# The second layer's two products: one loop over token spans, against two phases with the hidden values stored in DRAM between them

## The chip, the cores and the metric

The program runs on one core of a Trainium2 chip. The core has a matrix engine (TensorE, PE in the rows, with its weight loads as PEld), a vector engine (VectorE, DVE), a scalar engine (ScalarE, ACT), GpSimd (POOL) and the sync engine (SP), which issues the transfers between DRAM and on-chip memory. The metric is the device time in microseconds (us) of one execution.

## The reference, cut to what matters

```
x = attention(q, k, v)                   # 8 batches x 576 tokens; x is 4608 tokens x 512
h = maximum(x @ w1_in, 0);  x2 = (h * h) @ w1_out         # first layer, hidden width 2048
h = x2 @ w2_in;  g = maximum(0.01 * h, h)                 # second layer, hidden width 2048
out = g @ w2_out                                          # 4608 x 512
```

Only the last two lines are computed differently by the changed kernel. The weights arrive as 64-bit floats, and earlier code turns them into 32-bit words.

## The kernel before, in words

Every product is made of three passes in the PE's reduced 32-bit format: a value is rounded to a high part (a ScalarE copy), the low part is the difference (a VectorE subtraction), and high x high, low x high and high x low are added up in PSUM. I call the two steps "high" and "low" below.

The attention and the first layer run in blocks of 512 tokens. A background helper, `Stored`, converts the second layer's weights at the same time, a step per `tick` (L335), and stores them in DRAM: `w2_raw` for `w2_in`, and `w2_parts`, already split in high and low, for `w2_out`. The first layer's result goes to DRAM as `x2`.

The second layer (`Second`) starts when the last block of the first ends. A span is 768 tokens, seen as two halves of 384. Its first product is a Strassen-Winograd scheme: the 512 input columns, the 256 hidden columns of a "pair" and the 768 tokens are each cut in two, and 7 block products take the place of 8. `x_sum`, `x_high` and `x_low` make the 7 forms of x for a span, on tiles of 128x768; `make_in` makes the 7 forms of the weights of a pair. A group is one pair on one span: `product(g, j)` (L1310) is 6 matmuls of 384 columns, and `use` (L1328) drains it. The drains alternate over two PSUM banks, and product j accumulates on top of product j - 2, so it can start only when the drain of j - 2 has read the bank.

After each of the products 0 to 5 stands one `piece` (L1378) of the group before: 6 matmuls of 512 columns, for 128 tokens, of the second product. The leaky relu is a VectorE operation (L1358), and then high (L1362) and low (L1365) of the hidden values follow. On-chip memory holds the weights of 4 of the 8 pairs, so the spans are walked twice, forward for pairs 0 to 3 and backward for 4 to 7, and the result of the first walk goes through DRAM (`part`). That is 48 groups in all. When the span changes, the forms of the next span are made during the last pair (p = 3) and the first steps of the next group, one form after each product.

The order of the instructions on each engine is the order in which the code issues them; nothing reorders it. SP issues its transfers in that order too, at most 8 of them outstanding.

Of the kernel before, what the change touches and what calls it, by code (L numbers as in the profile page):

```python
# [43 lines left out]
def attention_relu2_leaky_kernel(  # L44
# [67 lines left out]
    w2_parts = dram.tile([FC // 2, P, 2, 1024], F32, tag="w2p", name="w2p")  # L112
    part = dram.tile([NT, DM], F32, tag="part", name="part")
# [101 lines left out]
    def half_words_of(w, kind, i, n):  # L215

        if kind == 0:
            src = w[2 * n * P : 2 * (n + 1) * P, 4 * i * P : 4 * (i + 1) * P]
            return (
                src.rearrange("(k p) f -> p k f", p=P),  # L220
                lambda t: t.rearrange("p (k f) w -> p k (f w)", k=2),
            )
        c = 2 * i + n
        return w[c * P : (c + 1) * P, :], lambda t: t.rearrange("p f w -> p (f w)")
# [94 lines left out]
    class Stored:  # L319
# [8 lines left out]
        def load(self, h):  # L328
            kind, i, n = h % 2, h // 4, h // 2 % 2
            src, to = half_words_of(self.w[kind], kind, i, n)  # L330
            t = sb([P, 512, 2], U32, "val")
            nc.sync.dma_start(out=to(t), in_=src)
            self.halves[h] = t[:, :, 0], t[:, :, 1]

        def tick(self):  # L335
# [18 lines left out]
            elif k == 4 and h % 2:  # L354
                t = sb([P, 2, 512], F32R, "val")
                nc.vector.tensor_copy(t[:, 0, :], self.out)
                nc.vector.tensor_tensor(
                    out=t[:, 1, :], in0=self.out, in1=f32(t[:, 0, :]), op=ALU.subtract
                )
                self.out = f32(t)  # L360
            elif k == 5 - (h + 1) % 2:
                i, n = h // 4, h // 2 % 2
                to = w2_parts[i, :, :, n * 512 : (n + 1) * 512] if h % 2 else w2_raw[i, :, n]
                nc.sync.dma_start(out=to, in_=self.out)
# [786 lines left out]

    TS = 384
    SPAN = 2 * TS
    SPANS = NT // SPAN
    TT = SPAN // P
    PAIRS = FC // 4
    A11, A12, A22, S1, S2, S3, S4 = range(7)
    FORMS = (A11, S2, A12, S3, S1, A22, S4)

    class Second:  # L1160
        def __init__(self):
            self.order = [(0, n) for n in range(SPANS)] + [(1, n) for n in reversed(range(SPANS))]
            self.groups = [(*o, p) for o in self.order for p in range(PAIRS)]
            self.weights, self.outs, self.late, self.begun = {}, {}, [], {}

        def open_forms(self):
# [3 lines left out]
            opened.insert(0, pool)  # L1170
# [7 lines left out]
        def open_work(self):  # L1178
            pool = tc.alloc_tile_pool(name="gs", bufs=1, side="right", reuse_waits="tile")
            opened.append(pool)  # L1180
            self.gh, self.gl = (
                [
                    [
                        [pool.tile([P, TS], F32R, tag=f"{n}{k}{c}{t}", name=n) for t in range(2)]
                        for c in range(2)
                    ]
                    for k in range(2)
                ]
                for n in ("sh", "sl")
            )  # L1190
            POOLS.update({"u3": pool, "h11": pool})
            BUFS.update({"u3": 2, "h11": 2})
            self.acc = [acc_bank(m) for m in range(KC)] + [bank() for _ in range(2)]
            self.banks = [bank() for _ in range(2)]
# [37 lines left out]
        def load_in(self, half, p):  # L1232
            i = PAIRS * half + p
            self.words = [sb([P, 2, 2, P], F32, "raw") for _ in range(2)]
            for n, t in enumerate(self.words):
                nc.sync.dma_start(out=t.rearrange("p k j f -> p (k j f)"), in_=w2_raw[i, :, n])

        def make_in(self, p):
            ra, rb = self.words
            sums = sb([P, 4, 2, P], F32, "sums")  # L1240
            s1, s2, s3, s4 = (sums[:, n] for n in range(4))
            hi = sb([P, 7, 2, P], F32R, f"wi{2 * p}")
            lo = sb([P, 7, 2, P], F32R, f"wi{2 * p + 1}")
# [25 lines left out]
        def fetch_out(self, half, p):  # L1269
# [226 lines left out]
```

## Time and profile before

| | us |
|---|---|
| median of 3 runs (1725.42 to 1729.01) | 1728.6 |
| the profiled execution | 1730.24 |
| its span, from first to last instruction | 1728.5 |
| PE busy in the span | 1695.7 |
| VectorE busy | 1110.4 |
| ScalarE busy | 626.5 |

The span is the time from the first to the last instruction; the execution takes 1.7 us more. The granted clock of the PE is 0.997 of full speed. The matmuls overlap, so a single one's length in the rows (337 ns for 384 columns) is longer than the step from one start to the next, and it is the steps that add up. The second layer takes the stretch from 979 us to the end.

### The profile page before, as it was taken

What the parts mean: (1) busy time and instruction counts of PE and PEld (TensorE: products, weight loads), DVE (VectorE), ACT (ScalarE), POOL (GpSimd) and SP (SyncE); (2) the same over time, 40 slices, a digit from 0 to 9 for tenths busy, and PEclk for the clock granted to TensorE, in tenths of its full rate; (3) what the DMA queues carried; (4) which work ended last, traced back from release to release, by engine and by line L of the source; (5) the groups of instructions that cost most, each with busy time, mean ns of one, the idle gap of its engine ahead of it and who ended that gap; (6) DMA issues with size and microseconds to landing.
All of it is one profiled execution on the core that took longest, in us unless ns stands there. A gap on an engine that the chain in (4) does not pass through costs nothing.

```text
span 1728.5 us, 21707 instructions
## 1 busy us (share of the span) xinstructions
PE 1695.7 (98%) x8312; PEld 1465.9 (85%) x8312; DVE 1110.4 (64%) x2020; ACT 626.5 (36%) x1496; POOL 19.4 (1%) x38
## 2 busy tenths in 40 slices
PE   6999999999999999999999999999999999999999
PEld 6778888888888888888888899999999999999997
DVE  7978886667656676665435565565566675666564
ACT  4545343343443433433433332332332332233221
POOL 0011000000000000000000000000000000000000
PEclk9999999999999999999999999999999999999999
DMA  8924542322223232232004202201202411330220
GB/s 224 336 93 162 173 135 95 101 97 95 77 100 109 85 98 79 83 113 74 19 29 161 80 1 74 74 16 58 74 31 92 171 60 51 110 109 8 104 74 37
DMA packets 106296, 162.44 MB, mean 94 GB/s; under 512 B 44112, under 2 KB 44240, under 8 KB 105168
## 3 DMA queue, kind: packets, MB, share of 16 engines
q1 hardware_dynamic: 103632, 152.67, 26.3%
q0 software_dynamic: 2560, 8.39, 1.3%
q8 instruction: 65, 1.06, 0.2%
q14 instruction: 39, 0.32, 0.1%
HBM read 111.75 MB, written 49.28 MB: 93 GB/s over the span
## 4 chain that ended last, share of the span: by engine, by line
PE 91%; DVE 4%; ACT 2%; DMA 2%; issue 1%; SPq 1%; DVEq 0%
PE acc L910 21%; PE ps L1317 20%; PE ps L872 17%; PE acc L1384 15%; PE ps L1384 8%; PE acc L872 4%; PE ps L587 2%; PE ps L650 1%; DMA wo<-in_moe_w_out 1%; DMA wi<-in_moe_w_in 1%; PE ps L551 1%; PE acc L381 1%; ACT s L608 1%; DVE xl L679 0%; PE ps L656 0%
## 5 line engine op out<-in xcount | busy, mean ns | idle before, releaser
L872 PE MATMUL ps<-xh,wi 128*128 128x512 f32 x896 | 296.5, 393 | 0.0
L1317 PE MATMUL ps<-fh,wi 128*128 128x384 f32 x1344 | 289.2, 337 | 0.1
L910 PE MATMUL acc<-gh,wo 128*128 128x512 f32 x1080 | 276.7, 394 | 0.7 <-ACT xl L882 0.7
L1317 PEld LDWEIGHTS ps<-fh,wi 128*128 128x128 f32 x1344 | 243.1, 188 | 22.2 <-DVE gh L1330 0.4
L910 PEld LDWEIGHTS acc<-gh,wo 128*128 128x128 f32 x1080 | 200.7, 189 | 41.8 <-ACT xl L882 1.2
L1384 PE MATMUL acc<-wo,sh 128*128 128x512 f32 x768 | 205.6, 390 | 0.0
L872 PEld LDWEIGHTS ps<-xh,wi 128*128 128x128 f32 x896 | 168.2, 188 | 34.6 <-issue 0.2
L872 PE MATMUL ps<-xl,wi 128*128 128x512 f32 x448 | 174.4, 389 | 0.0
L1317 PE MATMUL ps<-fl,wi 128*128 128x384 f32 x672 | 171.2, 336 | 0.0
L889 DVE CAST gh<-r 128x512 fp32r<-128x512 f32 x112 | 47.6, 425 | 174.5 <-ACT r L885 173.9
L1384 PEld LDWEIGHTS acc<-wo,sh 128*128 128x128 f32 x768 | 141.5, 188 | 15.6
L910 PE MATMUL acc<-gl,wo 128*128 128x512 f32 x540 | 149.6, 391 | 0.0
L882 ACT ACTIVATE r<-ps 128x512 f32<-128x512 f32 x112 | 67.7, 605 | 208.9 <-PE ps L872 204.6
L1317 PEld LDWEIGHTS ps<-fl,wi 128*128 128x128 f32 x672 | 121.4, 188 | 0.0
L1384 PE MATMUL acc<-wo,sl 128*128 128x512 f32 x384 | 120.3, 392 | 0.0
L910 PEld LDWEIGHTS acc<-gl,wo 128*128 128x128 f32 x540 | 101.8, 189 | 21.6
L608 ACT ACTIVATE s<-ps,m 128x72 f32<-128x72 f32 x240 | 72.1, 330 | 93.8 <-DVE m L599 93.7
L1330 DVE TENSOR_TENSOR u<-gh,ps 128x384 f32<-128x384 f32 x48 | 26.6, 554 | 120.1 <-PE ps L1317 120.1
L1384 PE MATMUL ps<-wo,sh 128*128 128x512 f32 x384 | 102.8, 390 | 0.0
L872 PEld LDWEIGHTS ps<-xl,wi 128*128 128x128 f32 x448 | 84.2, 188 | 16.5
L1384 PEld LDWEIGHTS acc<-wo,sl 128*128 128x128 f32 x384 | 72.0, 188 | 18.3 <-DVE sl L1365 3.7
L890 DVE TENSOR_TENSOR gl<-r,gh 128x512 fp32r<-128x512 f32 x112 | 77.6, 692 | 7.8 <-PE ps L656 0.5
(211 smaller groups left out, 2419.8 us busy)
## 6 DMA issues: line engine op xcount, KB each, us to landing
wi<-in_moe_w_in SPq DMA_DIRECT2D x8, 1024.0 KB
wo<-in_moe_w_out SPq DMA_DIRECT2D x8, 1024.0 KB
val<-in_moe_w_in SPq DMA_DIRECT2D x16, 512.0 KB
val<-in_moe_w_out SPq DMA_DIRECT2D x16, 512.0 KB
w2p<-val SPq DMA_DIRECT2D x16, 512.0 KB
wo<-w2p SPq DMA_DIRECT2D x8, 1024.0 KB
xh<-x SPq DMA_DIRECT2D x10, 768.0 KB
xl<-x SPq DMA_DIRECT2D x10, 768.0 KB
```

Source lines behind the costliest of these rows:

```text
L381: nc.tensor.matmul(ps[:n, c * 2 * D : (c + 1) * 2 * D], lhsT=ident[:n, :n], rhs=raw[:n, r * 2 * D : (r + 1) * 2 * D], start=r == 0, stop=r ...
L551: nc.tensor.transpose(ps[:, cc * P : (cc + 1) * P], raw[:, cc * P : (cc + 1) * P], ident)
L587: nc.tensor.matmul(ps[: r0 + n, c2 * PAIR : (c2 + 1) * PAIR], lhsT=qt[:, cc, : r0 + n], rhs=kts[b][:, keys], start=True, stop=True,)
L608: nc.scalar.activation(out=s[:, g, :], in_=ps[:, h * SP : (h + 1) * SP], func=AF.Exp, bias=m[:, g : g + 1], accum_out=None if i in early e ...
L872: nc.tensor.matmul(ps, lhsT=w[:, kc], rhs=x[kc], start=(kc == 0 and n == 0), stop=(kc == KC - 1 and n == 2),)
L882: nc.scalar.activation(out=r, in_=ps, func=AF.Relu)
L889: nc.vector.tensor_copy(gh, r)
L890: nc.vector.tensor_tensor(out=gl, in0=r, in1=f32(gh), op=ALU.subtract)
L910: nc.tensor.matmul(acc[m], lhsT=w[:, m * P : (m + 1) * P], rhs=x, start=(c == 0 and n == 0), stop=(c == FC - 1 and n == 2),)
L1317: nc.tensor.matmul(at, lhsT=w[:, FORMS[j], kc], rhs=x[j][:, kc], start=m == 0 and j in (0, 1, 4), stop=m == 5, skip_group_check=True,)
L1330: nc.vector.tensor_tensor(out=out_, in0=x, in1=at, op=ALU.add)
L1384: nc.tensor.matmul(self.acc[i], lhsT=x[g % 2][c][t][:, at], rhs=self.outs[p][:, part_, c], start=p == 0 and m == 0, stop=p == PAIRS - 1 an ...
```

## The change

The second layer is done in two phases. In phase 1 the six spans are walked once, over all 8 pairs (48 groups, p = 0 to 7), with the first product alone. The weights of pairs 4 to 7 go to the tiles of the first layer's `w_out`, and are made during the first five groups. The drains use two sets of three PSUM banks, set by set in turn. The leaky relu becomes ScalarE's Lrelu. No high and low of the hidden values are made here: five forms of them, two of which are sums made by VectorE (`sums_of`), go to DRAM (`h_forms`), 5 transfers of 192 KB a group.

In phase 2 the second product is a 7-product scheme too: hidden rows, the two token halves, and the two halves of the 512 output columns are cut. A round is 256 columns of the 2304-wide forms; 9 rounds of 8 groups are walked. A group loads 5 forms (640 KB), VectorE makes the other two, ScalarE makes the high and VectorE the low of all seven, and the PE does 7 products of 6 matmuls with 256 columns. The products accumulate over the 8 groups of a round in 7 of the 8 PSUM banks, and are drained in the last group of a round.

The forms of `w_out` are made by `Stored` (`w2_forms`, in place of `w2_parts`), loaded in the last span of phase 1 and split there, a pair per group, behind product 1 (`split_out`).

```diff
@@ Stored.tick, half of w_out
-                t = sb([P, 2, 512], F32R, "val")
-                nc.vector.tensor_copy(t[:, 0, :], self.out)
-                nc.vector.tensor_tensor(
-                    out=t[:, 1, :], in0=self.out, in1=f32(t[:, 0, :]), op=ALU.subtract
...
+                nc.sync.dma_start(out=to[:, 0:1], in_=o[:, 0, 0:1])
+                nc.sync.dma_start(out=to[:, 1:3], in_=o[:, 1])
+                t = sb([P, 4, P], F32, "val")
+                for at, x, y in (
+                    (t[:, 0:2], o[:, :, 1], o[:, 0]),
...
+            elif k == 5 and h % 2:
+                t, to = self.sums
+                nc.sync.dma_start(out=to[:, 3:7], in_=t)
@@ product, use
-            at = self.banks[(g + j) % 2][:, :TS]
+            at = self.banks[3 * (g % 2) + (0, 1, 0, 1, 2, 1, 2)[j]][:, :TS]
...
+            def leaky(out_, x):
+                nc.scalar.activation(out=out_, in_=x, func=AF.Lrelu)
...
-                self.leaky(self.u2, k, 0, 1)
-
-        def leaky(self, h, k, c, t):
-            nc.vector.scalar_tensor_tensor(
-                out=h, in0=h, scalar=0.01, in1=h, op0=ALU.mult, op1=ALU.max
-            )
...
+                leaky(self.u2, self.u2)
+                self.late.append(self.sums_of(g))
+
+        def sums_of(self, g):
...
+                s3 = sb([P, TS], F32, "st")
+                nc.vector.tensor_tensor(out=s3, in0=h11, in1=h21, op=ALU.subtract)
+                nc.vector.tensor_tensor(out=h21, in0=h21, in1=h22, op=ALU.add)
+                for at, x in ((H11, h11), (H12, h12), (H22, h22), (HS3, s3), (HS1, h21)):
+                    nc.sync.dma_start(out=to[:, at], in_=x)
@@ group
+                at = self.product(g, j)
+                if more and p == PAIRS - 2 and j in (1, 2, 4):
                     self.x_sum((1, 2, 4).index(j))
+                if more and p == PAIRS - 1:
                     if j >= 2:
                         self.x_low(j - 2)
                     if j == 4:
                         self.x_sum(3)
                     self.x_high(j)
+                if n and p == 0 and j < 2:
                     self.x_low(5 + j)
-                if g and j < 6:
-                    self.piece(g - 1, j)
...
+                if last and j >= 5:
+                    ends.append((j, at))
+                else:
+                    self.use(g, j, at)
+                for _ in range(1 + (j == 6)):
+                    if self.making:
+                        self.making.pop(0)()
+                if not more and p and j == 1:
+                    self.split_out(p - 1)
@@ phase 2
+        def prepare(self, g, parts):
...
+                for at, x, y in ((HS2, HS1, H11), (HS4, H12, HS2)):
+                    nc.vector.tensor_tensor(out=t[:, at], in0=t[:, x], in1=t[:, y], op=ALU.subtract)
...
+        def products(self, g):
...
+            steps = self.prepare(g + 2, (slice(0, 5), slice(5, 7)))
+            for j, (a, b) in enumerate(SECOND):
+                at = self.all_banks[(7 * r + j) % 8]
+                for s in range(2):
+                    for m, (x, w) in enumerate(((hi, wh), (hi, wl), (lo, wh))):
+                        nc.tensor.matmul(
+                            at[:, s * TR : (s + 1) * TR],
+                            lhsT=x[:, a, s * P : (s + 1) * P],
+                            rhs=w[:, b],
...
@@ run
+            for g in range(SPANS * PAIRS):
+                ends = self.group(g)
+            self.open_second()
+            self.load_second(1)
+            for step in self.prepare(0, [slice(n, n + 1) for n in (0, 1, 5, 2, 3, 4, 6)])[:-1]:
+                step()
+            for j, at in ends:
+                self.use(SPANS * PAIRS - 1, j, at)
             self.flush()
+            self.split_out(PAIRS - 1)
+            self.load_second(2)
+            self.load_second(3)
+            for step in self.prepare(1, (slice(0, 5), slice(5, 7))):
+                step()
```

How the order of the instructions moves is shown at three places. The first is the PE in the middle of the second layer, with products (`fh`, `fl` are the forms of x) and pieces (`sh`, `sl` are the hidden values) in turn, in the kernel before:

```order
L1317 MATMUL ps<-fh,wi_10805 128x384 x2
L1317 MATMUL ps<-fh,wi_10806 128x384 x2
L1317 MATMUL ps<-fl,wi_10805 128x384 x2
L1384 MATMUL ps<-wo_10755,sh 128x512 x4
L1384 MATMUL ps<-wo_10755,sl 128x512 x2
```

In the changed kernel the products of phase 1 follow each other (here 0 to 2 of the first group; `acc_8375` and `acc_8376` are banks):

```order
L1337 MATMUL acc_8375<-fh,wi_8080 128x384 x2
L1337 MATMUL acc_8375<-fh,wi_8081 128x384 x2
L1337 MATMUL acc_8375<-fl,wi_8080 128x384 x2
L1337 MATMUL acc_8376<-fh,wi_8080 128x384 x2
L1337 MATMUL acc_8376<-fh,wi_8081 128x384 x2
L1337 MATMUL acc_8376<-fl,wi_8080 128x384 x2
L1337 MATMUL acc_8375<-fh,wi_8080 128x384 x2
```

The 6 matmuls of 512 columns that stood between two products are gone from this place.

The second place is VectorE at a change of span (`fl` are the lows of the forms of x, `xl<-xl,t2` the last sum; L1330 drains a bank). Before, from the drain of product 1 on:

```order
L1330 TENSOR_TENSOR gl_9085<-gh_9070,ps_8341 128x384
L1365 TENSOR_TENSOR sl_8328<-gl_8978,sh_8320 128x384
L1227 TENSOR_TENSOR fl_7704<-xh_8853,fh_7697 128x768
L1330 TENSOR_TENSOR u3_9117<-gh_9070,ps_8341 128x384
L1358 SCALAR_TENSOR_TENSOR h11_9101<-h11_9101 128x384
L1227 TENSOR_TENSOR fl_7705<-t2_8997,fh_7698 128x768
L1330 TENSOR_TENSOR u3_9117<-u3_9117,ps_8342 128x384
L1358 SCALAR_TENSOR_TENSOR u3_9117<-u3_9117 128x384
L1365 TENSOR_TENSOR sl_8331<-h11_9101,sh_8323 128x384
L1227 TENSOR_TENSOR fl_7706<-xl_8855,fh_7699 128x768
```

In the changed kernel, behind the drain of product 1 and the sums L1387 and L1388 of the group before:

```order
L1388 TENSOR_TENSOR gl_8831<-gl_8831,r_8857 128x384
L1240 TENSOR_TENSOR fl_7768<-xh_8747,fh_7761 128x768
L1240 TENSOR_TENSOR fl_7769<-t2_8847,fh_7762 128x768
L1350 TENSOR_TENSOR r_8928<-gh_8891,ps_8379 128x384
L1240 TENSOR_TENSOR fl_7770<-xl_8749,fh_7763 128x768
L1230 TENSOR_TENSOR xl_8749<-xl_8749,t2_8847 128x2x384
L1350 TENSOR_TENSOR r_8928<-r_8928,ps_8380 128x384
L1240 TENSOR_TENSOR fl_7771<-xh_8747,fh_7764 128x768
L1350 TENSOR_TENSOR gh_8891<-gh_8891,ps_8379 128x384
```

The forms of x now stand ahead of the drain that belongs to the same product, two of them ahead of the drain of product 3.

The third place is VectorE between the phases (L1409 splits `w_out`, L1463 makes two forms, L1469 the lows that the first groups of phase 2 need):

```order
L1350 TENSOR_TENSOR r_11653<-r_11653,ps_8380 128x384
L1463 TENSOR_TENSOR xh_11637<-xh_11637 128x256 x2
L1469 TENSOR_TENSOR hl_11684<-xh_11637,hh_11679 128x256 x7
L1350 TENSOR_TENSOR gh_11613<-gh_11613,ps_8379 128x384
L1350 TENSOR_TENSOR gl_11621<-gl_11621,ps_8380 128x384
L1387 TENSOR_TENSOR st_11709<-r_11645,gl_11621 128x384
L1388 TENSOR_TENSOR gl_11621<-gl_11621,r_11653 128x384
L1409 TENSOR_TENSOR wo7_11718<-xl_11565,wo6_11717 128x768
L1409 TENSOR_TENSOR wo7_11718<-xl_11565,wo6_11717 128x1024
L1463 TENSOR_TENSOR hr_11687<-hr_11687 128x256 x2
L1469 TENSOR_TENSOR hl_11685<-hr_11687,hh_11680 128x1280
```

The last drains of phase 1 and the last split stand between the forms of the first and of the second group of phase 2.

## Rows read from the trace of the kernel before

**Rows 1.** The page's first part: busy us, share of the span and instructions of each engine.
```profile
PE 1695.7 (98%) x8312; PEld 1465.9 (85%) x8312; DVE 1110.4 (64%) x2020; ACT 626.5 (36%) x1496; POOL 19.4 (1%) x38
```
**Rows 2.** The chain of waits in order of time, 940 to 1728: start, length, what.
```profile
979.11 4.19 PE ps L1317 x24
...
1721.92 2.73 PE ps L1384 x12
```
**Rows 3.** Timeline of PE, 1300 to 1340: start, length, engine, line, tiles, shapes, count.
```profile
1312.62 0.86 PE L1317 MATMUL ps<-fh,wi 128*128 128x384 f32 x4
...
1313.66 1.07 PE L1384 MATMUL acc<-wo,sh 128*128 128x512 f32 x4
...
1328.10 0.86 PE L1317 MATMUL ps<-fh,wi 128*128 128x384 f32 x4
```
**Rows 4.** Timeline, 468.8 to 476.8: PE with 256 columns, first and last of 14.
```profile
474.95 0.28 PE L703 MATMUL ps<-ptl,v_hi 128*128 128x256 f32 x1
...
476.51 0.28 PE L704 MATMUL ps<-ptr,v_rem 96*128 96x256 f32 x1
```
**Rows 5.** Timeline, 781 to 790: PE with 64 columns, first and last of 12.
```profile
788.35 0.28 PE L701 MATMUL ps<-pth,v_hi 128*128 128x64 f32 x1
...
789.58 0.28 PE L704 MATMUL ps<-ptr,v_rem 96*128 96x64 f32 x1
```
**Rows 6.** Lines by form, 960 to 1728, VectorE: shapes, count, busy us, mean ns, idle before.
```profile
L1227 DVE TENSOR_TENSOR fl<-xl,fh 128x768 fp32r<-128x768 f32 x30 | 28.5, 950 | 0.0
...
L1330 DVE TENSOR_TENSOR u<-gh,ps 128x384 f32<-128x384 f32 x48 | 26.6, 554 | 120.1 <-PE ps L1317 120.1
...
L1252 DVE TENSOR_TENSOR wi<-sums,wi 128x1024 fp32r<-128x1024 f32 x6 | 7.3, 1220 | 0.4 <-ACT wi L1255 0.4
L1252 DVE TENSOR_TENSOR sums<-raw 128x256 f32<-128x256 f32 x12 | 4.5, 420 | 2.3 <-DMA raw<-w2r 2.3
```
**Rows 7.** The same view of ScalarE.
```profile
L1224 ACT CAST fh<-xl 128x768 fp32r<-128x768 f32 x30 | 25.0, 835 | 0.0
...
L1334 ACT COPY gh<-ps 128x384 f32<-128x384 f32 x48 | 22.7, 472 | 0.4 <-PE ps L1317 0.4
...
L1255 ACT CAST wi<-sums 128x1024 fp32r<-128x1024 f32 x6 | 6.3, 1048 | 3.9 <-DVE sums L1252 3.9
```
**Rows 8.** Timeline, 1088 to 1112: a product's drain behind the PE.
```profile
1103.62 1.07 PE L1384 MATMUL acc<-wo,sh 128*128 128x512 f32 x4
1103.82 0.55 DVE L1330 TENSOR_TENSOR u<-gh,ps 128x384 f32<-128x384 f32 x1 [2.34 <-PE ps L1317]
```
**Rows 9.** Timeline, 983.8 to 996: the first group, whose products have no pieces between.
```profile
985.90 0.55 DVE L1330 TENSOR_TENSOR gh<-gh,ps 128x384 f32<-128x384 f32 x1
...
986.50 0.64 PEld L1317 LDWEIGHTS ps<-fh,wi 128*128 128x128 f32 x4 [0.41 <-DVE gh L1330]
986.50 0.96 PE L1317 MATMUL ps<-fh,wi 128*128 128x384 f32 x4
```
**Rows 10.** Timeline, 1312.0 to 1328.2: SP's issues and the work that waits for them.
```profile
1311.76 0.32 SPq L1271 DMA_DIRECT2D wo<-w2p  x1
1312.13 0.90 SPq L1236 DMA_DIRECT2D raw<-w2r  x2
...
1318.13 0.76 DVE L1252 TENSOR_TENSOR sums<-raw 128x256 f32<-128x256 f32 x2 [0.78 <-DMA raw<-w2r]
```
**Rows 11.** Transfers by line: queue, operation, count, KB each, median us to landing.
```profile
mid<-r POOLq DMA_DIRECT2D x20, 256.0 KB, 2.6
```
**Rows 12.** Lines of ScalarE, 0 to 40: the load of its function table.
```profile
L556 ACT ACT_TABLE_LOAD x1 | 1.3, 1283 | 0.7 <-PEq L1475 0.7
```
**Rows 13.** Windows: PE busy (count), PEld, DVE, ACT, POOL, clock, DMA share, GB/s.
```profile
300.00:500.00 200.00, 197.82 (x966) 164.86 (x965) 132.98 (x271) 82.36 (x245) 0.00 (x0) 1.00 0.29 94
```
**Rows 14.** Waits of SP's queue: who waited for whom, us in total, times, longest.
```profile
SPq L332 <- DMA w2p<-val: 15.6, 6, 4.3
```
**Rows 15.** The tile of the results: the issues of its stores, first and last start.
```profile
L1399 SPq DMA_DIRECT2D out<-raw x18: 332/332/338, 1412.9 to 1725.4; - x18
```

More of the change, by code (lines that the diff above doesn't have):

```diff
@@ L1401, in group, with load_out, split_out @@
-        def group(self, g):
-            half, n, p = self.groups[g]
-            after = self.groups[g + PAIRS - p][1] if g + PAIRS - p < len(self.groups) else n
-            before = self.groups[g - p - 1][1] if g > p else n
-            swap = (half, n) == (0, SPANS - 1)
-            steps = []
+        def load_out(self, p):
+            t = self.landed[p] = sb([P, 7, TR], F32, ("xh", "xl")[p % 2])
+            nc.sync.dma_start(out=t, in_=w2_forms[p])
+        def split_out(self, p):
+            t = self.landed.pop(p)
+            hi, lo = (sb([P, 7, TR], F32R, tag) for tag in self.slots(p))
+            self.outs[p] = hi, lo
+            for at in (slice(0, 3), slice(3, 7)):
+                nc.scalar.copy(hi[:, at], t[:, at])
+                nc.vector.tensor_tensor(out=lo[:, at], in0=t[:, at], in1=f32(hi[:, at]), op=ALU.subtract)
@@ L1407, in group @@
+        def group(self, g):
+            n, p = divmod(g, PAIRS)
+            more, last = n + 1 < SPANS, g == SPANS * PAIRS - 1
+            ends = []
             for j in range(7):
-                self.product(g, j)
-                if after != n and p == 2 and j in (1, 2, 4):
+                at = self.product(g, j)
+                if more and p == PAIRS - 2 and j in (1, 2, 4):
                     self.x_sum((1, 2, 4).index(j))
-                if after != n and p == 3:
+                if more and p == PAIRS - 1:
@@ L1416, in group @@
                     self.x_high(j)
-                if before != n and p == 0 and j < 2:
+                if n and p == 0 and j < 2:
                     self.x_low(5 + j)
-                if g and j < 6:
-                    self.piece(g - 1, j)
-                if swap and p or (half, n, p) == (1, SPANS - 1, 0):
-                    if j == 2:
-                        steps = self.make_in((p - 1) % PAIRS)
-                    for step in steps[: 10 if j == 6 else 2]:
-                        step()
-                    steps = steps[2:]
@@ L1427, in group @@
-            if swap and p or (half, n, p) == (1, SPANS - 1, 0):
-                self.fetch_out(1, (p - 1) % PAIRS)
-            if swap:
-                self.load_in(1, p)
-            if p == 0 and after != n:
-                self.load_x(after, ("xh", "xl"))
-            if half and p == PAIRS - 1:
-                for i in range(TT):
-                    st = self.begun[i] = self.result_tile(i)
-                    nc.sync.dma_start(out=st, in_=part[self.rows(n, i), :])
-        def run(self):
-            opened.pop().release()
-            self.open_work()
-            for g in range(len(self.groups)):
-                self.group(g)
-            self.flush()
-            for i in range(TT):
-                self.piece(len(self.groups) - 1, i)
+                if last and j >= 5:
+                    ends.append((j, at))
+                else:
+                    self.use(g, j, at)
```

247 lines of the change are left out of this document (151 added, 96 removed).

## The prediction

> **What bounds the kernel now.** I read the page's busy times first: the PE works 98% of the span [rows 1]. Then the chain of waits: from 979.11, when the second layer's first product begins, to 1724.65 (the last matmuls start at 1721.92 and take 2.73) it runs almost only through the PE [rows 2]. That stretch is 745.5 us. The timeline gives its rhythm [rows 3]: a product takes 1.04 (1312.62 to 1313.66), and a whole group, 7 products and 6 pieces, 15.48 (1312.62 to 1328.10). 48 groups are 743.0, so PE's waits in the stretch come to 2.5. The reader is to see that VectorE and ScalarE have no part in the time here: a bank drained by one of them is wanted again only a piece and a product later. The one place without pieces is the first group, and there the PE does wait once: the drain at 985.90 ends at 986.45, and the PE, idle for 0.41, resumes at 986.50 [rows 9].
>
> **What the PE gains.** The pieces go: 15.48 - 7 x 1.04 = 8.20 a group, 48 x 8.20 = 393.6. The 336 products stay. Added are 9 x 8 x 42 = 3024 matmuls of 256 columns. The trace has such ones in the attention: 13 steps from 474.95 to 476.51, 0.120 each [rows 4]. 3024 x 0.120 = 362.9. The gain is 30.7. A step of 0.119 or 0.121 moves this by 3 either way.
>
> At this place the Trainium skill speaks against the change: "TensorE: Matmul & The Clock Gate", section "Back-to-back issue gap", gives 81 ns for 128 columns and 131 ns for 512 in a sustained stream of loads and matmuls. By that, 256 columns would take an estimated 98 ns, the new product 296 us and the old one (1728 x 0.131) 226 us: 70 us lost. The trace disagrees: a matmul of 512 columns takes 8.20 / 36 = 0.228 here, and one of 64 still 0.112 (11 steps from 788.35 to 789.58) [rows 5]. The sum goes by the rows.
>
> **What the PE will wait for.** In phase 1 nothing stands between the products. Product j accumulates in the bank of an earlier one (1 then 3 then 5, 4 then 6, 0 then 2) and cannot start before that one is drained, so a drain has one product's time, 1.04, less the 0.20 from the PE's end to the drain's start (1103.62 to 1103.82) [rows 8] and 0.05 back to the PE, whose first four matmuls then take 0.96 [rows 9] instead of 0.86 [rows 3]. A drain lasts 0.55 [rows 6], the ScalarE copy 0.47 [rows 7]. Undisturbed, that fits: 0.55 + 0.20 + 0.15 = 0.90 of 1.04. But 0.14 is all the slack, and whatever VectorE has ahead of a drain in its queue is added. I walked through the groups with these durations; back to back, operations overlap by 0.08 (two of 0.42 take 0.76 [rows 10]), so 384 columns occupy VectorE for 0.47, 768 for 0.87 and 1024 for 1.14 [rows 6].
>
> *Change of span, five times.* In group p = 7 VectorE has 5 drains, 2 sums, 5 lows and a sum of x: 7 x 0.47 + 6 x 0.87 = 8.5 us of work for 7.3 of PE. By order: on ScalarE the high of form 0 (0.84) stands ahead of the copy of product 0, which ends at 2.5 after the group's start; product 2 starts 0.5 late. The drain of product 1 ends at 3.1, then come two sums and two lows (0.94 + 1.74), and the drain of product 3 ends at 6.4: product 5, due at 5.7, waits 0.7. Another low and the last sum (1.74) stand ahead of the drain of product 4, which ends at 8.6: product 6, due at 7.5, waits 1.1. That is 2.3; the group after pays 0.7 for the last two lows, the one behind it about 0.3, and p = 6 with its three sums of x 0.4. 3.7 per change, 18.4 in all. Bounds: 0, if VectorE makes the lows in gaps; and 26, if the PE waits for each of the six forms of p = 7 (6 x 0.87 x 5).
>
> *Split of w_out, seven times.* Behind product 1 in the last span stand two sums, then a low of 768 and one of 1024 (0.94 + 0.87 + 1.14). The drain of product 3 ends at 6.4, and product 5 was due at 5.2: 1.2 each, 8.4 in all. Bounds: 0 (5.9 of 7.3 is VectorE's sum) and 2.0 each.
>
> *First groups and first load of x.* `make_in` runs on during five groups; in two of them its rounding of 1024 columns (1.05 [rows 7]) delays the copy of product 0 by about 1 us each. The load of x for the second span can start only when these groups are done with its tiles, and the store of h11 stands behind its 1.5 MB; that tile is the next u3, so a drain waits, about 2.0. With 0.4 of smaller ones: 4.5. Lrelu needs one table load, 1.28 [rows 12], in the first group, where ScalarE has the time. Lrelu itself is not in the trace: it costs at least the 0.47 of a copy and hardly over the 0.55 of a drain; I take 0.51. A duration of 0.8 would cost 5 us.
>
> *Between the phases.* The load for the first group of phase 2 needs the tile that the split of pair 6 frees at 5.8 in the last group. 1 MB and 2 x 256 KB land within 6.37 (1311.76 to 1318.13) [rows 10] and 256 KB in 2.6 [rows 11]: 348 GB/s and 1.85 fixed. 640 KB is there about 4.1 after its issue, at 9.9, when the PE has been done since 8.5; two sums and a low later, near 11.4, it starts: 2.9. Then VectorE has 6 lows (2.0), two drains and two sums (1.9), the last split (2.0), two sums of the next group (0.7) and its low of 1280 (1.4, from the 1024's rate): 8.0 and a little waiting for ScalarE, while the PE's first group lasts 42 x 0.120 = 5.04. 3.7 more. Together 6.6; between 2 (if the load is early) and 11.
>
> *Inside phase 2* I find no wait. VectorE needs 2 x 0.34 + 1.40 + 0.60 = 2.7 of each 5.04; in the last group of a round 7 drains of 0.60 more, 6.9, which overruns by 1.9, but a bank is wanted again 8 products (5.76) later, so this cover holds. ScalarE needs 1.9. Loads are 655 KB per 5.04, 130 GB/s; stores in phase 1 983 KB per 7.3, 135 GB/s, both well under the 348. Their rows are 1 to 1.5 KB, which the trace does not show alone; I take 336 GB/s for them, and keep 250 as the other end (13 us more, by the same walk).
>
> *First layer.* `Stored` makes three subtractions of 512 columns in all where a copy and a subtraction of 512 stood, and more, smaller transfers. PE is busy 197.8 of 200 there [rows 13]; SP's queue has waited up to 15.6 in all for such stores [rows 14] without holding the PE. Bounds: -6 (what PE idles there) and +15.6; I take 0.
>
> *The sum.* Waits: 18.4 + 8.4 + 4.5 + 6.6 = 37.9, where 2.5 were. -30.7 + 37.9 - 2.5 = +4.7. The end is alike: before, the last store is issued 0.7 behind the last matmul, at 1725.4 [rows 15], and the span ends 3.1 later; after, two stores and a drain a little late make it about 0.4 longer. +5.1 on the profiled execution's 1730.2 is 1735.3. That execution lies 1.6 above the median of the runs, so the forecast is 1733.7, rounded 1734.
>
> **The rivals.** *A: the drains keep up.* VectorE and ScalarE could take the forms of x and the split in the gaps they have (VectorE idles 120 us before one of its drains alone [rows 6]), so that neither the change of span nor the split delays a product. Then 26.8 of waits go: 1733.7 - 26.8 = 1707, faster. For it: the sums of work over p = 6, 7 and 0 (8.5 + 5.9 + 5.0) are under three groups' 21.9. Against it: queues run in order, and the lows stand ahead of the drain by construction. It decides when these two waits come to under 21.7 instead of 26.8 (1733.7 - 1728.6 = 5.1 less): there the change breaks even. Half of them gone gives 1720.
>
> *B: the transfers become the bound.* Stores and loads in rows of 1 to 1.5 KB at 250 GB/s: the load of x holds the stores of h11 at each change, and drains wait for tiles: 1747. At 200 it is 1769. For it: 47 MB of hidden values go out and come back, where `part` took 9.4 each way. Against it: 256 KB in 2.6.
> The Trainium skill, "DMA: Bandwidth & Descriptors", section "Bandwidth", lists 138 GB/s for 64 KB and 341 for 1 MB; stores of 192 KB at 138 would fill 7.1 of a group's 7.3. Rows 11 do not go that far: 256 KB with all fixed time is 101 GB/s, and several are under way at a time.
>
> *C: narrow matmuls pay for their weights.* If each of the 3024 took the mean weight load, 1465.9 / 8312 = 0.176 [rows 1], 169 us would be added: 1903. The steps of 0.112 and 0.120 speak against it. The skill's 131 ns of above would end on this side too.
>
> **How the numbers follow.** Forecast, 1729 to 1742: 0.62. A, whole or half: 0.24. B: 0.12. C: 0.02. A measurement of this kernel tells about 0.2% (3.5 us) from no change. Under 1725.1 lie 0.18 of A and 0.02 of the forecast: faster 0.20. Within: 0.06 of A and 0.16 of the forecast: 0.22. Slower: 0.58. The range takes in half of A's gain and B at 250 GB/s: 1717 to 1750.
>
> **What would show it.** Steps of 0.120 in phase 2 and 1.04 in phase 1 where nothing waits; PE idle before products 2, 5 and 6 at p = 7, some 2.3 a group, with VectorE's drain as releaser; 1.2 before product 5 in the last span; two gaps of about 3 at the start of phase 2; none later. It is wrong if PE idles under 30 or over 45 in the second layer, if a 256-column step is not 0.120, or if drains wait for stores at every group.

## The result and the profile after

The changed kernel takes 1743.55 us (median of 4 runs, 1741.57 to 1744.75); the kernel before, run beside it, takes 1727.01. The ratio is 1.0094, 95% interval 1.0077 to 1.0112: slower by 16.5 us. The forecast was 1734, that is 5.1 slower than before. The sign was right and the size was not.

The profiled execution took 1743.6, with a span of 1741.8. The page's busy times, to be read against [rows 1]:

```profile
PE 1676.7 (96%) x9608; PEld 1501.6 (86%) x9608; DVE 1155.6 (66%) x2029; ACT 710.8 (41%) x1552; POOL 19.6 (1%) x39
```

The PE is busy 19 us less, and the span is 13.3 longer: the PE waits 32 us more. First the part that came out as worked out. Windows of the changed kernel (length, busy time and count of PE, PEld, DVE, ACT, POOL; clock; DMA share; GB/s), one inside phase 2:

```profile
1400.00:1500.00 100.00, 100.00 (x835) 100.00 (x834) 67.66 (x98) 36.11 (x42) 0.00 (x0) 1.00 0.46 146
```

835 matmuls in 100.00 us are 0.120 each, as in [rows 4], and the view of waits names none of the PE's between 1400 and 1735. The gain of 30.7 is there.

Then a change of span. Timeline of PE through group p = 7 of the third span; it starts at 1160.11 and the next group, on the weights `wi` again, at 1169.91: 9.80 where an unhindered group takes 7 x 1.04 = 7.28.

```profile
1160.11 0.86 PE L1337 MATMUL acc<-fh,wo 128*128 128x384 f32 x4
...
1162.58 0.97 PE L1337 MATMUL acc<-fh,wo 128*128 128x384 f32 x4 [0.22 <-ACT gh L1357]
...
1166.43 0.97 PE L1337 MATMUL ps<-fh,wo 128*128 128x384 f32 x4 [0.46 <-DVE r L1350]
...
1168.75 0.97 PE L1337 MATMUL ps<-fh,wo 128*128 128x384 f32 x4 [1.01 <-DVE r L1350]
1169.91 0.34 PE L1337 MATMUL acc<-fh,wi 128*128 128x384 f32 x1
```

The waits are before products 2, 5 and 6, released by ScalarE's copy and by VectorE's drains. VectorE in the same group shows why: a form and a sum stand ahead of the drain of product 4.

```profile
1166.29 0.95 DVE L1240 TENSOR_TENSOR fl<-xl,fh 128x768 fp32r<-128x768 f32 x1
1167.28 0.96 DVE L1230 TENSOR_TENSOR xl<-xl,t 128x768 f32<-128x768 f32 x1
1168.15 0.55 DVE L1350 TENSOR_TENSOR r<-r,ps 128x384 f32<-128x384 f32 x1
```

In the last span the split of `w_out` stands ahead of the drain of product 3, and product 5 waits for it, 1.11 in each of seven groups. Timeline of PE, the last of them:

```profile
1361.98 0.97 PE L1337 MATMUL ps<-fh,wo 128*128 128x384 f32 x4 [1.11 <-DVE r L1350]
```

What was not expected in this size: drains that wait for a store. Timeline of the changed kernel behind the load of x for the fourth span:

```profile
1108.82 0.43 SPq L1216 DMA_DIRECT2D xh<-x  x1
1109.35 0.45 SPq L1216 DMA_DIRECT2D xl<-x  x1
...
1109.90 0.41 SPq L1390 DMA_DIRECT2D hf<-r  x1
...
1118.87 0.55 DVE L1350 TENSOR_TENSOR r<-gh,ps 128x384 f32<-128x384 f32 x1 [3.38 <-DMA hf<-r]
```

The store of H11 is issued at 1109.90, right behind 1.5 MB of x in the same queue. Its tile, one of three called `r`, is the u3 of the next group, and the drain into it waits until 1118.87. There was no such store before the change. The PE waits behind this drain, and then runs at half clock for a while (timeline of PE, and a window):

```profile
1119.48 1.65 PE L1337 MATMUL ps<-fh,wi 128*128 128x384 f32 x4 [2.57 <-DVE r L1350]
...
1121.56 1.41 PE L1337 MATMUL ps<-fh,wi 128*128 128x384 f32 x4
...
1123.16 0.86 PE L1337 MATMUL acc<-fh,wi 128*128 128x384 f32 x4
```
```profile
1119.00:1123.00 4.00, 3.52 (x12) 3.52 (x13) 1.53 (x3) 1.05 (x2) 0.00 (x0) 0.57 0.05 17
```

The two products from 1119.48 to 1123.16 take 3.68 instead of 2.08.

Between the phases the timeline of PE shows four waits, and the windows what follows them:

```profile
1366.37 0.50 PE L1485 MATMUL acc<-wi,hh 128*128 128x256 f32 x2 [2.02 <-ACT hh L1466]
1367.13 0.39 PE L1485 MATMUL acc<-wi,hl 128*128 128x256 f32 x1 [0.26 <-DVE hl L1469]
...
1373.46 0.50 PE L1485 MATMUL acc<-wi,hh 128*128 128x256 f32 x2 [1.27 <-ACT hh L1466]
1376.01 0.58 PE L1485 MATMUL acc<-wi,hl 128*128 128x256 f32 x1 [2.05 <-DVE hl L1469]
1376.39 0.63 PE L1485 MATMUL acc<-wi,hh 128*128 128x256 f32 x2
...
1382.15 0.42 PE L1485 MATMUL ps<-wi,hh 128*128 128x256 f32 x2
```
```profile
1376.00:1378.00 2.00, 1.99 (x9) 1.99 (x10) 0.56 (x1) 0.00 (x0) 0.00 (x0) 0.50 1.08 379
1378.00:1380.00 2.00, 2.00 (x11) 2.00 (x11) 1.50 (x3) 1.78 (x3) 0.00 (x0) 0.50 1.10 353
1380.00:1382.00 2.00, 2.00 (x12) 2.00 (x11) 1.97 (x4) 1.26 (x1) 0.00 (x0) 0.50 0.57 181
1382.00:1384.00 2.00, 2.00 (x18) 2.00 (x18) 2.00 (x3) 1.61 (x2) 0.00 (x0) 0.96 0.47 132
```

After the PE had idled twice, the granted clock is 0.50 (1.2 GHz) for six microseconds: the 27 steps from 1376.39 to 1382.15 take 5.76 instead of 3.24.

The first layer is shorter: the second begins at 973.87 instead of 979.11 [rows 2]. Of these 5.2, 3.4 are the profile of before, in which the clock fell at two more places of the first layer, and not the change:

```profile
108.00:110.00 2.00, 2.00 (x7) 1.78 (x6) 0.88 (x2) 0.54 (x1) 0.00 (x0) 0.50 0.00 0
684.00:688.00 4.00, 4.00 (x13) 3.12 (x13) 1.49 (x4) 1.17 (x2) 0.00 (x0) 0.64 0.27 101
```

In the profile of after both stretches have 1.00. The other 1.9 arise in the first 37 us, by the starts of the same matmuls in both; no view names a reason. The part on why the prediction was wrong shows that such a difference comes without any change.

### The profile page after: what moved, and what is told of

It is laid out like the page before. It is cut to its first block, busy times and chain, and to the rows that moved or that the text cites. A ratio compares the mean times of both kernels' runs of the same rounds, so it can differ in the third digit from the quotient of the medians.

```text
span 1741.8 us, 25310 instructions
## 1 busy us (share of the span) xinstructions
PE 1676.7 (96%) x9608; PEld 1501.6 (86%) x9608; DVE 1155.6 (66%) x2029; ACT 710.8 (41%) x1552; POOL 19.6 (1%) x39
## 5 line engine op out<-in xcount | busy, mean ns | idle before, releaser
L1485 PE MATMUL acc<-wi,hh 128*128 128x256 f32 x512 | 95.9, 287 | 3.3 <-ACT hh L1466 3.3
L1337 PE MATMUL acc<-fh,wo 128*128 128x384 f32 x432 | 94.5, 341 | 3.5 <-DVE r L1350 2.2
L1337 PE MATMUL acc<-fh,wi 128*128 128x384 f32 x432 | 94.2, 340 | 3.3 <-ACT gh L1357 1.7
L1485 PE MATMUL acc<-wo,hh 128*128 128x256 f32 x512 | 93.8, 283 | 0.0
L1485 PE MATMUL ps<-wi,hh 128*128 128x256 f32 x496 | 91.5, 284 | 0.0
L1485 PE MATMUL ps<-wo,hh 128*128 128x256 f32 x496 | 90.9, 283 | 0.0
L1485 PEld LDWEIGHTS acc<-wi,hh 128*128 128x128 f32 x512 | 81.5, 196 | 3.8 <-ACT hh L1466 3.8
L1337 PEld LDWEIGHTS acc<-fh,wo 128*128 128x128 f32 x432 | 75.4, 188 | 9.1 <-DVE r L1350 6.0
L1337 PEld LDWEIGHTS acc<-fh,wi 128*128 128x128 f32 x432 | 75.6, 188 | 8.3 <-ACT gh L1357 3.9
L1485 PEld LDWEIGHTS acc<-wo,hh 128*128 128x128 f32 x512 | 79.9, 192 | 0.0
```

The lines of the kernel that those rows point to most:

```text
L1337: nc.tensor.matmul(at, lhsT=w[:, FORMS[j], kc], rhs=x[j][:, kc], start=m == 0 and j in (0, 1, 4), stop=m == 5, skip_group_check=True,)
L1485: nc.tensor.matmul(at[:, s * TR : (s + 1) * TR], lhsT=x[:, a, s * P : (s + 1) * P], rhs=w[:, b], start=p == 0 and s == 0 and m == 0, stop= ...
```

## The experiments

The theory: the lost time lies in single waits, each made by what stands ahead of an urgent instruction in one queue. The rivals: VectorE has too much work for any order; transfers are near their limit; the clock falls whatever is done. "A group's excess" below is its length by the starts of PE's products, less 7.28. Times are medians, to be held against 1743.6 for the changed kernel and 1727 to 1728.5 for before; the ratio is to before, with its interval.

**e1_drain_first: the drain ahead of the forms of x.**
```
-  x_sum / x_low / x_high of this product;  self.use(g, j, at)
+  self.use(g, j, at);  x_sum / x_low / x_high of this product
```


> In group() the drain of a product is put ahead of the forms of x that are made behind the same product; nothing else changes. Theory (order in VectorE's queue): the waits of the group p = 7, 2.5 us in the changed kernel, fall to about 0.5, because a drain no longer has a form of 0.95 us ahead of it; part comes back at p = 0, where the last lows now fall between drains (0.8 becomes about 2). Together some 1.3 us less in each of five changes of span: 1736 to 1739 us against 1743.6. Rival (amount of work): VectorE has 8.5 us of work in a group of 7.3, whatever the order; all of the wait moves to p = 0 and the time stays within 2 us of 1743.6.


1743.3, ratio 1.0083 (1.0066 to 1.0100): nothing won, as the rival had it. The excess at p = 7 fell from 2.5 to 0.55, at p = 6 it rose from 0.55 to 1.25 and more, at p = 0 from 0.7 to between 2.2 and 3.8: a late drain there makes Lrelu late, and behind Lrelu and a high of x on ScalarE stands the copy of product 0.

```profile
1048.19 1.43 PE L1337 MATMUL acc<-fh,wi 128*128 128x384 f32 x4 [1.91 <-ACT gh L1357]
```

**e2_x_load_gpsimd: loads of x from another queue.**
```
-  nc.sync.dma_start(out=t, in_=src...)
+  (nc.gpsimd if n else nc.sync).dma_start(out=t, in_=src...)
```


> The loads of x for spans 1 to 5 (2 x 768 KB each) are issued from GpSimd's queue, idle there, and no longer stand in SP's queue ahead of the stores of the hidden values. Theory (one queue, first in first out): the four waits of VectorE for stores of r (8.6 us, longest 3.4) go, and the PE's 2.24 and 2.57 us in the groups (span 0, p = 5) and (span 2, p = 1) with them; about 6 us faster, 1737 to 1739. Rival (shared DMA engines): the 1.5 MB and the stores share the 16 engines whichever queue issues them; stores land as late, and the time stays within 1.5 us of 1743.6.


1735.6, ratio 1.0044 (1.0029 to 1.0059): 8 us won. No drain waits for a store any more; the one at the place shown above now waits for the PE alone:

```profile
1114.46 0.55 DVE L1351 TENSOR_TENSOR r<-gh,ps 128x384 f32<-128x384 f32 x1 [0.41 <-PE ps L1338]
```

From the first product of phase 1 to the start of the last, the changed kernel takes 389.3 and this one 380.3. So in these profiles the stores behind loads cost 9.0, 1.6 of it by the half clock shown above. The Trainium skill, "Trainium Kernel Development and Optimization", section "Key Constraints", says that issuing from several engines only saves the sequencer's issue time, since all queues share 16 DMA engines. Here the measurement differs: what was saved is the place of a store behind 1.5 MB. The Trainium skill's page "DMA: Bandwidth & Descriptors", section "Queues, rings and completion order", fits the row better: an engine takes packets from its queues in turn. No run here shows these turns by themselves.

**e13_h11_tile: the other remedy.** The load stays where it was, H11 gets another tile.
```
-  self.h11 = sb([P, TS], F32, "r")
+  self.h11 = sb([P, TS], F32, "raw")
```


> The changed kernel with one edit: H11 lies in the tiles called raw (three, free in phase 1) instead of sharing the three called r with u3. The loads of x stay in SP's queue, ahead of stores. Theory (a store behind a load costs time only because the next drain wants the stored tile): the waits of VectorE for stores of r go, as in e2_x_load_gpsimd, 7 to 8 us faster, 1736. Rival (the stores themselves, or the load, hold the work up by the queue): a drain waits in another place and less than 3 us are won.


1736.7, ratio 1.0051 (1.0037 to 1.0066): 6.8 won, and phase 1 takes 380.3 as in e2. A late store costs nothing by itself; it costs where its tile is wanted. Each of the two conditions, queue and tile, was needed. VectorE in the same place:

```profile
1116.88 0.55 DVE L1350 TENSOR_TENSOR r<-gh,ps 128x384 f32<-128x384 f32 x1 [0.41 <-PE ps L1337]
```

**e3_split_spread: the split of w_out in single forms.**
```
-  at j == 1: split_out(p - 1); load_out(p + 1)
+  highs behind j = 0, 2; lows behind j = 1, 3, 4, 5, 6; load_out(p + 1) behind j = 6
```


> The split of the second weights in groups p = 1 to 6 of the last span is cut into single forms: highs behind products 0 and 2, lows of one form behind products 1, 3, 4, 5, the last three behind product 6; the last group is as it was. Theory (order in VectorE's queue): VectorE has 5.9 us of work in a group of 7.3, and a low of 0.35 fits into the 0.49 it idles between two drains; the wait of 1.11 before one product goes in these six groups with the slower start behind it (1.38 a group): 8.3 us faster, 1735. Rival (the drains have no slack at all): each low delays the drain behind it and the waits come back in smaller parts; under 3 us faster.


1763.6, ratio 1.0197 (1.0172 to 1.0222): 20 slower. Neither theory had it, and the cause is the edit's other half: the load of 0.9 MB now goes out just ahead of a store of H11, and the same wait as above comes in the split groups from the second on, 2.6 to 3.6 each on the PE. The profiled execution took 1756.5, 7 less than the median, so it shows only part of the loss. In e5_combined that load has another queue, and these waits are gone.

```profile
1312.64 0.32 SPq L1401 DMA_DIRECT2D xh<-w2f  x1
...
1313.01 0.43 SPq L1390 DMA_DIRECT2D hf<-r  x1
...
1318.66 0.55 DVE L1350 TENSOR_TENSOR r<-gh,acc 128x384 f32<-128x384 f32 x1 [3.38 <-DMA hf<-r]
```

**e4_start_order: the start of phase 2 in another order.**
```
-  prepare(0); drains 5, 6; flush; split_out(7); loads 2, 3; prepare(1)
+  drains 5, 6; prepare(0) by forms with the split between; loads 2, 3; prepare(1); flush
+  the first load in two parts; group 0 takes the two made forms last
```


> The start of phase 2 in another order: the last two drains of phase 1 come first, the first load of hidden values lands in two parts and its five loaded forms are taken before the two made ones, the last split of weights lies in VectorE's gaps, and the last two sums and stores of phase 1 come behind the parts of group 1. Theory (load and VectorE order; the clock fell because the PE had idled): the PE's idle time between 1364 and 1376, some 6 us with the lows, falls to about 2.5, the granted clock stays at 1.0, and the 22 matmuls at half clock (about 2.7 us) go: 6 us faster, 1736 to 1739. Rival (the clock falls at this place whatever the idle time): 3 us faster, and rows with a granted clock of 0.5 remain.


1740.8, ratio 1.0070 (1.0055 to 1.0085): 2.8 won of 6. The PE still waits 1.64 and 1.85, and the clock is 0.62 behind the second wait, for a shorter time.

**e5_combined: e2, e3 with its loads on GpSimd's queue, and e4 with group 1 by forms.**
```
+  load_out: nc.gpsimd.dma_start(...)
+  prepare(1, single forms); in group 7: split_out(6) ahead of flush
```


> Three edits together: the loads of x from GpSimd's queue; the split of the second weights in single forms as in e3_split_spread, but with the loads of these weights on GpSimd's queue, so that they don't stand ahead of the stores of hidden values (there a drain waited 3.38 us for a store); and the start of phase 2 as in e4_start_order, with group 1 made form by form like group 0 and the last split ahead of two sums. Theory (each wait is one queue's order): 8.0 from the loads, 6 x 1.38 = 8.3 from the splits, some 6 at the start of phase 2, together 22: 1721. Rival (the waits have one common cause, VectorE's total work, and come back elsewhere): over 1730.


1724.0, ratio 0.9978 (0.9969 to 0.9987): 19.6 won, a little faster than before. The split groups have no excess but 0.49 in the first, and 1.40 in the last, whose split was left whole; so a low of one form does fit between two drains. The clock stays at 1.00 at the start of phase 2, though the PE waits 1.64, 0.54 and 1.02 there:

```profile
1360.00:1364.00 4.00, 2.44 (x19) 2.03 (x18) 3.52 (x7) 2.88 (x3) 0.00 (x0) 1.00 1.04 354
```

**e6_sums_gpsimd: two sums of hidden values on GpSimd.**
```
-  nc.vector.tensor_tensor(out=s3, ...); nc.vector.tensor_tensor(out=h21, ...)
+  nc.gpsimd.tensor_tensor(out=s3, ...); nc.gpsimd.tensor_tensor(out=h21, ...)
```


> The two sums of hidden values of each group (S3 and S1, 384 columns each) run on GpSimd; all else as in the changed kernel. VectorE has 0.94 us less ahead of the drain of product 3 in every group. Theory (work ahead of a drain in VectorE's queue): 0.94 of the 1.11 in seven split groups and about as much in five groups p = 7: 11 us faster, 1732. Rival (GpSimd is slow at such sums, or takes VectorE's access to memory): VectorE's drains take longer than 0.55, or the stores of S3 and S1 come so late that drains wait for their tiles; no gain, or slower than 1743.


1739.5, ratio 1.0066 (1.0051 to 1.0081): 4.1 won of 11. The wait in a split group fell from 1.11 to 0.56, at p = 7 the excess from 2.5 to 1.9. But a sum takes 1.02 there, and the next drain, whose tile it reads, waits for it; VectorE stood so for 46.6 us in 28 waits. Most are hidden; at p = 0 one reaches the PE, and the excess there rose from 0.7 to 1.5.

```profile
1305.39 1.02 POOL L1387 TENSOR_TENSOR st<-r,gl 128x384 f32<-128x384 f32 x1 [5.35 <-ACT gl L1353]
1306.45 0.55 DVE L1350 TENSOR_TENSOR gl<-gh,ps 128x384 f32<-128x384 f32 x1 [1.69 <-POOL st L1387]
```

**e7_leaky_vector: the leaky step back on VectorE.**
```
-  nc.scalar.activation(out=out_, in_=x, func=AF.Lrelu)
+  if j == 2: nc.scalar.copy(out_, x)
+  nc.vector.scalar_tensor_tensor(out=out_, in0=out_, scalar=0.01, in1=out_, op0=ALU.mult, op1=ALU.max)
```


> The leaky steps go back from ScalarE's Lrelu to VectorE's scalar_tensor_tensor, the one of H11 behind a copy on ScalarE; all else as in the changed kernel. Theory (VectorE's queue): four more operations of 0.47 a group; a split group then has 7.8 us of VectorE's work in 7.3, a group p = 7 10.4 and the first groups about 2 more each: some 15 to 25 us slower, about 1763. Rival (VectorE is busy 66% and has room): under 4 us slower.


1764.6, ratio 1.0205 (1.0190 to 1.0221): 21 slower, as worked out; the wait in a split group is 1.58. In phase 1, where nothing stands between the products, Lrelu on ScalarE is worth 21 us.

**e12_lrelu_before: that part alone, in the kernel before.** The same exchange of lines there, the other way.


> The kernel before with one part of the change alone: its leaky step is ScalarE's Lrelu in place of VectorE's scalar_tensor_tensor. Theory (there the PE's queue of products and pieces sets the time, and VectorE and ScalarE are off the path): within 2 us of the kernel before. Rival (VectorE's share matters there too): over 3 us faster.


1725.6 against 1728.45, ratio 0.9981 (0.9971 to 0.9992): 2.8 us faster, between what the theory and the rival gave. In its trace the stretch from the first product to the last pieces is 740.9 (979.69 to 1720.54), 2 less than [rows 2]: that is most of the 2.5 that the PE waited before.

**e8_double_loads and e9_extra_stores: is there room for transfers?**
```
e8  +  for _ in range(2 if g > 2 else 1): nc.sync.dma_start(out=t[:, :5], in_=h_forms...)
e9  +  nc.gpsimd.dma_start(out=more_out[g], in_=t[:, :5])
```


> Every load of hidden values in phase 2 from the fourth on is issued twice into the same tile: 1.31 MB instead of 0.66 per group of 5.04 us, 260 GB/s. Theory (loads have room; the trace shows no wait in phase 2): within 4 us of 1743.6. Rival (transfers in rows of 1 KB are near their limit): a group takes longer than 5.04; at 200 GB/s 6.6 us, 69 groups and some 105 us slower.


1880.3. This run says nothing on the limit: the second load goes into the tile of the first and is held until that one has landed. Timeline of SP, two issues that stretch over 7.38:

```profile
1504.79 7.38 SPq L1454 DMA_DIRECT2D hr<-hf  x2
```


> The changed kernel with one more transfer per group of phase 2: the 640 KB that were just loaded are also stored to a spare DRAM tensor, from GpSimd's queue, each to a place of its own; no transfer waits for another's tile as in e8_double_loads. 1.31 MB per 5.04 us, 260 GB/s. Theory (transfers have room): within 4 us of 1743.6 and groups of 5.04. Rival (205 GB/s, which e8_double_loads moved, is the limit of such rows): a group takes 6.4 us, about 95 us slower.


1744.1, ratio 1.0085 (1.0065 to 1.0105): no change. The window shows twice the traffic of the changed kernel and a PE without a gap, so rival B has no hold in phase 2:

```profile
1400.00:1500.00 100.00, 100.00 (x835) 100.00 (x835) 67.35 (x98) 36.38 (x42) 10.70 (x20) 1.00 0.86 292
```

**e11_turn_order: only the order in p = 6, 7 and 0.**
```
p = 6, 7:  flush behind product 0, ahead of the first drain; x_sum / x_low behind the drains of 3, 4
p = 7:     Lrelu of products 5, 6 behind the next group's copy of product 0
p = 0:     x_low(5) behind product 1, x_low(6) behind product 4
```


> Only the order in which the operations of the groups p = 6, p = 7 and p = 0 stand in the queues of VectorE and ScalarE is another: the two sums of the group before come ahead of the first drain, where VectorE idles; the drains of products 3 and 4, whose banks are wanted again two products later, go ahead of forms of x; those of 5 and 6, whose banks are wanted a group later, and their Lrelu go behind more urgent work; two lows lie between the drains of p = 0. No operation is added or left out. Theory (which work stands ahead of an urgent drain): of the 3.7 us per change of span (0.4 + 2.5 + 0.8) some 0.5 is left, 16 us less in five changes: 1728. Rival (VectorE has 8.5 us of work in the 7.3 of p = 7, in whatever order): the waits only move, as in e1_drain_first; 1740 or more.


1736.7, ratio 1.0048 (1.0033 to 1.0063): 7 won of 16. The excess of p = 6, 7, 0 did fall from 3.8 to 0.94 (0.25, 0.43, 0.26): the order decides, not the amount of work. But the waits for the store of H11, 9.0 in all in the changed kernel, grew to 14. One of them, in VectorE's timeline and the PE's:

```profile
1056.08 0.55 DVE L1350 TENSOR_TENSOR r<-gh,ps 128x384 f32<-128x384 f32 x1 [2.76 <-DMA hf<-r]
...
1056.69 1.07 PE L1337 MATMUL ps<-fh,wi 128*128 128x384 f32 x4 [1.96 <-DVE r L1350]
```

**e14_queue_and_turn: e2 and e11 together.**
```
+  the edits of e2_x_load_gpsimd and e11_turn_order
```


> The loads of x from GpSimd's queue (e2_x_load_gpsimd) and the order of e11_turn_order together. Theory (two separate causes; alone, e11_turn_order lost half of its gain because its quicker groups met the stores behind the load of x): 8 and 14 us add up, 1743.6 - 22 = 1722, and no wait over 1 us is left in the groups p = 0 and 1 of spans 1 to 5. Rival (a change of span costs some 4 us however it is ordered): 1730 or more.


1725.4, ratio 0.9985 (0.9975 to 0.9994): 18 won of the 22. All groups p = 0, 6, 7 have 0.27, 0.26, 0.43, and p = 1 none in four of five spans. In the last span a wait of 2.08 is left, and there the load of w_out still stands ahead of the stores. Alone the two edits won 8.0 and 6.9, together 18.1: the order gives its whole gain only once the stores no longer stand behind the load.

**e10_more_order and e15_best.**
```
e10 = e5 + e11 + the first load of phase 2 ahead of the stores of pair 6 + group 2 by forms
      + the rounding of 1024 columns in the first groups cut in two
e15 = e10 without that cut, with the first two loads of phase 2 from nc.gpsimd
```


> e5_combined with the order of e11_turn_order, the rounding of 1024 columns in the first groups cut in two, the first load of phase 2 issued ahead of the stores of pair 6, and group 2 of phase 2 made form by form. Theory (queues' order): 16 from the change of span, 2 from the first groups, 3 at the start of phase 2 off the 1724.0 of e5_combined: 1703. Rival (the waits move): over 1718.


1713.3, ratio 0.9912 (0.9898 to 0.9927): 10.7 of the 21 expected over e5. The cut of the rounding won nothing (groups p = 1, 2, 3 of the first span have 0.80, 1.62 and 0.61, before 1.31, 1.09 and 0.00). The load put ahead of the stores made the known wait once more, 4.91 on the PE, and half clock behind it:

```profile
1337.74 1.65 PE L1339 MATMUL ps<-fh,wo 128*128 128x384 f32 x4 [4.91 <-DVE r L1352]
```
```profile
1336.00:1340.00 4.00, 2.26 (x7) 2.26 (x8) 1.11 (x2) 1.12 (x3) 0.00 (x0) 0.51 1.00 323
```


> e10_more_order with the first two loads of phase 2 from GpSimd's queue too, where they stood ahead of a store whose tile a drain wanted (a wait of 4.91 and a granted clock of 0.5 behind it), and without its cut of the rounding in the first groups, which won nothing. Theory (again a store behind a load): the 4.91 and the slower matmuls behind go, about 6 us off 1713.3: 1707. Rival (the load is simply late, whichever queue): within 2 us of 1713.


1710.9, ratio 0.9894 (0.9876 to 0.9911): 16.7 us faster than before and 32.7 faster than the changed kernel; 2.4 of the 6 expected of the last edit are seen. No wait in its second layer is over 1.11, and the clock has no fall between 1328 and 1360. It is the fastest kernel measured here.

## Why the prediction was right in sign and wrong in size

On the profiled executions +5.1 was forecast and +13.4 came (1743.6 against 1730.2). By its steps:

| step of the prediction | taken | measured | from |
|---|---|---|---|
| pieces against 256-column steps | -30.7 | -30.7 | 0.120 a step in phase 2 |
| change of span, five times | 18.4 | 19.0 | 5 x (0.55 + 2.52 + 0.72), e13 |
| split of w_out, seven times | 8.4 | 9.7 | 7 x 1.38 |
| first groups, without the load | 2.5 | 3.2 | 0.47 + 1.30 + 1.08 + 0.36 |
| stores of H11 behind loads of x | 2.0 | 9.0 | 389.3 - 380.3, e2 and e13 |
| between the phases, and the clock | 6.6 | 9.5 | 1364.18 to 1736.56, less 3024 x 0.120 |
| the end | 0.4 | 1.4 | 5.2 behind the PE's last matmul, 3.85 before |
| first layer | 0 | -5.2 | 973.87 against 979.11 |
| the PE's waits before, which go | -2.5 | -2.5 | 745.5 - 743.0, [rows 2] and [rows 3] |

*The step that failed* stands in "first groups and first load of x": "the store of h11 stands behind its 1.5 MB; that tile is the next u3, so a drain waits, about 2.0." The mechanism was seen, and counted once, for the second span, where it cost 2.5. It comes at every load of x, and cost 4.3 in one group (p = 1 of the third span, shown above). 2.0 was taken and 9.0 measured. By the table the second layer was taken too short by 13.4 in all; 7.0 of these are this term. Its size varies: 1.6 of the 9.0 is the half clock in that group, and in e8_double_loads and e9_extra_stores, whose phase 1 is the changed kernel's, the same groups lose 6.4 and 6.7.

*The second miss* is the clock. The two gaps between the phases were forecast at 2.9 and 3.7 and measured at 2.3 (2.02 + 0.26) and 3.3 (1.27 + 2.05). What was left out is that the PE starts again at half clock: 5.76 - 3.24 = 2.5.

Counted by lost steps, as the prediction's sum counts them, the waits of the second layer come to 50.4 (19.0 + 9.7 + 3.2 + 9.0 + 9.5), over the 45 that it named as a sign of being wrong; the idle time of the PE alone, by the view of waits, is 30.2. Two readings were off by little: the 0.41 of [rows 9] is idle time of the weight loads (PEld), and no wait of the PE is shown there; and by the stated 348 GB/s and 1.85 a load of 640 KB lands 3.7 after its issue, not 4.1.

*What held.* The waits before products 2, 5 and 6 at p = 7 come in their places with 0.22, 0.46 and 1.01 (0.5, 0.7 and 1.1 were taken); the split gave 1.11 for 1.2; Lrelu takes 0.53 from SBUF and 0.49 from PSUM for the 0.51 taken; no wait in phase 2. That VectorE's order, not its load, decides was the text's case against rival A; e11 shows it, and shows too that A needs only another order: its 26.8 of waits fell to 4.8 for the five changes of span (5 x 0.97) and 1.4 for the splits in e15, whose other repairs bring it to 1710.9. Rival B's price was right in kind for phase 1 (a load ahead of stores) and wrong in its reason, a rate of transfers: e9 moves 292 GB/s without harm. Rival C is excluded by the 0.120.

*The first layer* was taken as 0, and no run speaks against that. Of its 5.2, 3.4 are the clock in the profile of before, which took 1730.2 where later runs have medians of 1727.0 to 1728.5; so the medians lie 15 to 16.5 apart, more than the two profiles. The experiments on the changed kernel leave its first layer as it is, and in their profiles the second layer begins at times from 973.99 to 979.28; the profile of the changed kernel, with 973.87, is the earliest of all. In e15_best, where the clock fell at the same places as in the profile of before, it begins as late as before:

```profile
979.28 0.96 PE L1338 MATMUL acc<-fh,wi 128*128 128x384 f32 x4 [0.20 <-ACT st L937]
```

So the -5.2 is the luck of one execution, and it hid a part of what the second layer lost.

## What to carry to other kernels

Where a large load is issued ahead of small stores in one queue, look up who next writes the stored tiles: either another queue for the load or one more tile for the store took the whole wait away here. Between products that follow each other without a filler, give the drains the first place by the date at which their bank is wanted again, not by the order in which work is made; moving them blindly ahead (e1) only moved the wait. After each repair look for the wait that the quicker part runs into (e11, e10), since half of a gain went there.

## What the runs showed of the hardware

The granted clock fell to 0.5 after some waits of the PE and not after others of the same length. In e1_drain_first the wait of 1.91 shown above came in five groups; the two windows below follow it in the second span (the group lasted 3.75 too long), the third is the same place two spans later (2.20 too long).

```profile
1046.00:1050.00 4.00, 2.09 (x8) 1.81 (x7) 3.97 (x8) 2.06 (x4) 0.00 (x0) 0.81 0.28 98
1050.00:1053.00 3.00, 3.00 (x14) 3.00 (x14) 1.22 (x2) 0.49 (x1) 0.00 (x0) 0.69 0.93 254
...
1175.00:1179.00 4.00, 3.19 (x18) 3.19 (x19) 3.74 (x6) 1.25 (x3) 0.00 (x0) 1.00 0.43 128
```

So after the same wait of 1.91 a group was 2.2 or 3.8 too long. The runs do not show what decides. In the changed kernel the lone waits of 1.11 in the split groups were not followed by a fall; in e7_leaky_vector two waits of 1.11 and 1.00 in one group were (timeline of PE, and windows):

```profile
1041.82 0.98 PE L1337 MATMUL ps<-fh,wo 128*128 128x384 f32 x4 [1.11 <-DVE r L1350]
...
1044.15 1.56 PE L1337 MATMUL ps<-fh,wo 128*128 128x384 f32 x4 [1.00 <-DVE r L1350]
```
```profile
1040.00:1044.00 4.00, 2.03 (x11) 1.39 (x9) 3.97 (x6) 1.38 (x3) 0.00 (x0) 1.00 0.28 100
1044.00:1048.00 4.00, 3.85 (x13) 3.85 (x14) 3.90 (x8) 1.39 (x2) 0.00 (x0) 0.57 0.14 48
```
